# Four column orders for the streamed operand and the PSUM tile of the dense layers, chosen by chunk

## The chip, the cores and the metric

The kernel runs on one core of one Trainium2 chip. The metric is the device time of one launch in microseconds (us), the median of several executions. TensorE (PE in the profile) multiplies matrices, VectorE (DVE), ScalarE (ACT) and GpSimd (POOL) work on rows, and 16 DMA engines move data. A matmul on PE is two instructions: a weight load (LDWEIGHTS, PEld in the profile) puts one operand into the array, and the matmul streams the other operand past it, column by column, and adds the products up in a tile of PSUM.

## What is computed

Two layers of linear attention and two dense layers alternate on one sequence of 2048 rows with 576 features. The change touches the dense layers only, which the reference writes so:

```
def _B_ref(x, w1, b1, w2, b2):
    h = jnp.einsum("bsd,df->bsf", x, w1) + b1
    zero = jnp.zeros_like(h)
    r = jnp.where(h > zero, h, zero)
    h = r * r
    out = jnp.einsum("bsf,fd->bsd", h, w2) + b2
    return out
...
    x = x + _A_ref(_layernorm(x, axis=-1), A_wqkv, A_w_phi, A_wo)
    x = x + _B_ref(_layernorm(x, axis=-1), B_w1, B_b1, B_w2, B_b2)
```

The two lines at the end are run twice. w1 is 576 x 4608, w2 is 4608 x 576.

## The kernel before

The sequence is cut into four blocks of 512 rows (TB). For each layer and block the generator `g_mlp` computes the dense layer, eight times in all. It goes through the 4608 hidden features in NF = 36 chunks of 128, numbered f.

For precision every operand is held as a high and a low part in the type fp32r, and a product is summed from three matmuls (high by high, low by high, high by low). For chunk f this gives 29 matmuls:

- `hidden(f, cols)`, L979, 14 matmuls: the weights are a 128 x 128 piece of w1, the streamed operand is 128 x 512 of the normalised rows, transposed (`x["h"]`, `x["l"]`). They add up in the PSUM tile `ph` (named m_0ph to m_3ph by block), 128 x 512. In the first block of a layer (`apart`), chunks 0 and 1 are done in two halves of 256 columns.
- `square(f)`, L991 to L997: ACT adds the bias, clips and squares `ph` into `hr`, DVE splits the result into the high and low part `hb`.
- `by_rows(f, ts)`, L1017, 12 matmuls: for each of four row tiles t the weights are 128 x 128 of `hb`, and the streamed operand is 448 columns (R) of the chunk's rows of w2 (`s2`). They add up over all 36 chunks in the PSUM tile `acc[t]`.
- `features(f)`, L1005, 3 matmuls with 512 columns: the remaining 128 of the 576 output columns, into the fifth tile `acc[KC]`. The change does not touch them.

In the steady part the order on PE is hidden(f), then by_rows(f-1) and features(f-1), so that `square(f)` runs while PE does the products of the chunk before. Between two chunks `weave` lets pieces of the next block's attention in. Each engine takes its instructions in the order in which the program was written (`manual_schedule`), and the weights arrive by DMA from SP's queue one chunk ahead.

Three matmuls outside the dense layers matter below, since their operands aren't one unbroken run of columns. L587 (`kv_tile`) streams `zeros`, eight runs of 36 columns that all read the same 36 values, into an unbroken output of 288 columns. L617 (`key_totals`) streams two runs of 18 columns and writes two runs of 18; L611 beside it streams and writes 126 in one run. L494 (`project`) has 288 columns in one run.

Of the kernel before, what the change touches and what calls it, by code (L numbers as in the profile page):

```python
# [21 lines left out]
def layers_kernel(  # L22
# [18 lines left out]
    nc = tc.nc  # L41
# [7 lines left out]
    KC = D // P  # L49
# [864 lines left out]
    def g_mlp(layer, b, x, after, name, fresh, apart, final):  # L914

        acc, parts, raw2 = [], {}, {}
        R = D - P
# [41 lines left out]
        def bank(f):  # L959
            parts[f] += (ps_w.tile([P, TB], F32, tag="w", name=f"{name}ph{f}") if f == 1 else  # L960
                         ps_a.tile([P, TB], F32, tag="h", name=f"{name}ph{f}"),)

        def hidden(f, cols):
            if len(parts[f]) == 3:
                bank(f)
            h1, l1, s2, ph = parts[f][:4]
            xh, xl = x["h"], x["l"]
            todo = []
            for c in range(NC):
                ops = [(0, h1[:, c], xh[:, c, cols]), (1, l1[:, c], xh[:, c, cols])]  # L970
                if c < KC:
                    ops.insert(1, (0 if cols == every else 2, h1[:, c], xl[:, c, cols]))
                if c == KC and cols != every:
                    ops = [(3, *op[1:]) for op in ops]
                todo += ops
            if fresh or cols != every:
                todo.sort(key=lambda op: op[0])
            for k, (_, a, m) in enumerate(todo):
                nc.tensor.matmul(ph[:, cols], a, m, start=(k == 0), stop=(k == 3 * KC + 1))  # L979

        def square(f, cols=None, by_act=True):
            if len(parts[f]) == 4:
# [24 lines left out]
        def by_rows(f, ts):  # L1007
            if len(parts[f]) == 3:
                s2, hh, hl = parts[f]
            else:  # L1010
                s2, hb = parts[f][2], parts[f][5]
                hh, hl = hb[:, :TB], hb[:, TB : 2 * TB]
            hi, lo = s2[:, :R], s2[:, D : D + R]
            for t in ts:
                rows = slice(t * P, (t + 1) * P)
                for k, (a, m) in enumerate(((hh, hi), (hh, lo), (hl, hi))):
                    nc.tensor.matmul(acc[t][:, :R], a[:, rows], m, start=(f == 0 and k == 0),  # L1017
                                     stop=(f == NF - 1 and k == 2))

        def sums():  # L1020
# [2 lines left out]
        def second(f):  # L1023
            if not acc:
                sums()
            by_rows(f, range(NT // 2 if apart and f == 0 else 0, NT))
            features(f)
            del parts[f]

        halves = (slice(0, TB // 2), slice(TB // 2, TB))  # L1030
        if apart:
            if fresh:
                for f in range(3):
                    load(f)
            for f in range(2):
                first(f, nc.gpsimd)
                first2(f, nc.gpsimd)
            yield
            for f in range(2):
                hidden(f, halves[0])  # L1040
                if f == 0:
                    square(0, halves[0], False)
                yield
            sums()
            by_rows(0, range(NT // 2))
            for f in range(2):
                hidden(f, halves[1])
                square(f, None if f else halves[1])
            yield
            yield  # L1050
        else:
            for f in range(2):
                first(f)
                first2(f)
                hidden(f, every)
                square(f)
                yield
# [7 lines left out]
        for f in range(2, NF):  # L1065
            if fresh and f + 2 < NF:
                load(f + 2)
            if f + 1 < NF:
                first(f + 1)
            hidden(f, every)  # L1070
            square(f)
            yield
            if final and f == NF - 1:
                features(f - 1)
                by_rows(f - 1, range(NT - 1))
            else:
                second(f - 1)
            if f + 1 < NF:
                first2(f + 1)
            yield  # L1080
# [404 lines left out]
    def body():  # L1485
# [3 lines left out]
        for layer in range(2):  # L1489
            q1 = None  # L1490
            ready, prev_rows, keep = {}, None, {}
            for i, b in enumerate(order):
                n = f"{layer}_{b}"
                nxt, rows = {}, []
                gen = g_mlp(layer, b, ready, rows, f"m{n}", layer == 0 and i == 0, i == 0, layer == 1 and i == NB - 1)
                plan = Plan()
                if i == 0:
# [115 lines left out]
```

## Time and profile before

| what | value |
|---|---|
| median of three runs | 2489.95 us (2489.04 to 2490.05) |
| the profiled execution, its own time | 2489.11 us |
| its span, first to last instruction | 2487.4 us |
| outside the span | 1.7 us |
| PE weight load busy | 2177.9 us (88%) |
| DVE, ACT, POOL busy | 1275.0, 792.1, 307.6 us |
| DMA, mean share and rate | 59.5% in the hardware queue, 220 GB/s of HBM reads and writes |

A row of a view names line, engine, operation, output and inputs, shape and count; then the busy time in us, the mean duration of one in ns, and the idle time before. PE's durations overlap: a matmul's row runs on while the next one has begun, so what a matmul costs is the step from its start to the next start, and the duration is longer than that. In the view in order of time, neighbours with the same names are merged into one row with a count. A shape 128\*128 128x512 is 128 weight rows and columns, and a streamed operand of 128 partitions with 512 columns.

### The profile page before, as it was taken

Reading aid. Unit: us, or ns where it says so; the run is one execution under the profiler, and the core shown is the slowest. Engines: PE = TensorE matmul, PEld = TensorE weight load, DVE = VectorE, ACT = ScalarE, POOL = GpSimd, SP = SyncE. Lnnn points to the kernel's source line nnn. Section 1 sums busy time; section 2 is a strip of 40 time slices with the busy share of each in tenths; the row PEclk is TensorE's granted clock in tenths of the full one; section 3 lists DMA queues with packets and bytes.
Section 4 is the critical chain, followed back from the end, with each engine's and each line's share of the span. In section 5 each row is a group of like instructions: output and inputs, shape, how many; then the busy total and the mean of one; then the engine's idle time right before and its main releaser. Section 6 shows DMA issues by size and latency. Waiting matters only on the chain.

```text
span 2487.4 us, 37668 instructions
## 1 busy us (share of the span) xinstructions
PE 2472.3 (99%) x14924; PEld 2177.9 (88%) x14924; DVE 1275.0 (51%) x2234; ACT 792.1 (32%) x1439; POOL 307.6 (12%) x709
## 2 busy tenths in 40 slices
PE   9999999999999999999999999999999999999999
PEld 8999888889888888888888988888888888888887
DVE  6678885545744476455113776433553436442112
ACT  5444553423232223233223332312232222312212
POOL 4211210110302112020000022010110103020000
PEclk9999999999999999999999999999999999999999
DMA  9312698996767677595555248668576767666555
GB/s 318 102 54 92 238 310 276 318 339 214 259 234 274 222 235 265 208 325 169 194 197 172 97 152 271 207 216 289 178 256 210 259 222 244 218 225 232 194 198 170
DMA packets 177733, 550.57 MB, mean 221 GB/s; under 512 B 24302, under 2 KB 54478, under 8 KB 177558
## 3 DMA queue, kind: packets, MB, share of 16 engines
q1 hardware_dynamic: 163638, 500.44, 59.5%
q0 software_dynamic: 13920, 47.72, 5.9%
q8 instruction: 118, 1.93, 0.3%
q14 instruction: 57, 0.47, 0.1%
HBM read 441.95 MB, written 106.14 MB: 220 GB/s over the span
## 4 chain that ended last, share of the span: by engine, by line
PE 92%; DMA 3%; DVE 2%; POOL 1%; ACT 1%; issue 1%; SPq 0%; DVEq 0%; POOLq 0%; ACTq 0%
PE m_1ph L979 9%; PE m_2ph L979 9%; PE m_0ph L979 9%; PE m_3ph L979 8%; PE m_1acc L1017 7%; PE m_2acc L1017 7%; PE m_0acc L1017 7%; PE m_3acc L1017 6%; PE m_2acc L1005 2%; PE m_1acc L1005 2%; PE m_0acc L1005 2%; PE m_3acc L1005 2%; PE a_0po L817 1%; PE a_2po L817 1%; DMA a_1e<-phs 1%; PE kvp L594 1%
## 5 line engine op out<-in xcount | busy, mean ns | idle before, releaser
L979 PE MATMUL m_2ph<-a_2nh,m_2h 128*128 128x512 f32 x720 | 224.3, 393 | 2.2 <-DMA m_2h<-dw 2.2
L979 PE MATMUL m_0ph<-a_0nh,m_0h 128*128 128x512 f32 x720 | 224.2, 393 | 0.0
L1017 PE MATMUL m_0acc<-m_0s,m_0hb 128*128 128x448 f32 x864 | 189.4, 367 | 0.1
L1017 PE MATMUL m_3acc<-m_3s,m_3hb 128*128 128x448 f32 x864 | 189.4, 367 | 0.0
L1017 PE MATMUL m_1acc<-m_1s,m_1hb 128*128 128x448 f32 x864 | 189.2, 367 | 0.0
L1017 PE MATMUL m_2acc<-m_2s,m_2hb 128*128 128x448 f32 x864 | 189.0, 367 | 0.0
L996 DVE CAST m_2hb<-m_2hr 128x512 fp32r<-128x512 f32 x72 | 31.1, 432 | 287.9 <-ACT m_2hr L992 287.9
L1017 PEld LDWEIGHTS m_1acc<-m_1s,m_1hb 128*128 128x128 f32 x864 | 161.8, 188 | 18.0
L1017 PEld LDWEIGHTS m_0acc<-m_0s,m_0hb 128*128 128x128 f32 x864 | 161.3, 188 | 17.8 <-DVE m_0hb L997 0.8
L1017 PEld LDWEIGHTS m_3acc<-m_3s,m_3hb 128*128 128x128 f32 x864 | 161.3, 188 | 17.3
L1017 PEld LDWEIGHTS m_2acc<-m_2s,m_2hb 128*128 128x128 f32 x864 | 161.4, 188 | 17.1
L979 PEld LDWEIGHTS m_2ph<-a_2nh,m_2h 128*128 128x128 f32 x720 | 135.2, 188 | 33.5 <-issue 2.6
L996 DVE CAST m_1hb<-m_1hr 128x512 fp32r<-128x512 f32 (+1 forms) x73 | 30.9, 423 | 259.2 <-ACT m_1hr L992 259.1
L979 PEld LDWEIGHTS m_0ph<-a_0nh,m_0h 128*128 128x128 f32 x720 | 135.2, 188 | 30.6
L991 ACT ACTIVATE m_2hr<-m_2ph,b1t 128x512 f32<-128x512 f32 x72 | 49.6, 689 | 337.8 <-PE m_2ph L979 331.3
L991 ACT ACTIVATE m_1hr<-m_1ph,b1t 128x512 f32<-128x512 f32 (+1 forms) x72 | 49.4, 686 | 322.1 <-PE m_1ph L979 317.2
L991 ACT ACTIVATE m_0hr<-m_0ph,b1t 128x512 f32<-128x512 f32 x72 | 49.6, 689 | 312.1 <-PE m_0ph L979 312.1
L996 DVE CAST m_0hb<-m_0hr 128x512 fp32r<-128x512 f32 x72 | 31.4, 436 | 211.6 <-ACT m_0hr L992 211.5
L991 ACT ACTIVATE m_3hr<-m_3ph,b1t 128x512 f32<-128x512 f32 (+1 forms) x72 | 49.3, 685 | 213.0 <-PE m_3ph L979 213.0
L996 DVE CAST m_3hb<-m_3hr 128x512 fp32r<-128x512 f32 (+1 forms) x73 | 32.2, 441 | 163.9 <-ACT m_3hr L992 163.9
L979 PE MATMUL m_3ph<-t0onh,m_3h 128*128 128x512 f32 (+1 forms) x380 | 112.9, 384 | 0.7 <-ACT m_3hr L991 0.4
L979 PE MATMUL m_0ph<-a_0nl,m_0h 128*128 128x512 f32 x288 | 113.2, 393 | 0.0
(2089 smaller groups left out, 5861.6 us busy)
## 6 DMA issues: line engine op xcount, KB each, us to landing
m_2h<-dw SPq DMA_DIRECT2D x72, 640.0 KB
m_0h<-dw SPq DMA_DIRECT2D x72, 640.0 KB
m_1h<-dw SPq DMA_DIRECT2D x72, 640.0 KB
m_2s<-dw SPq DMA_DIRECT2D x72, 576.0 KB
m_0s<-dw SPq DMA_DIRECT2D x72, 576.0 KB
m_1s<-dw SPq DMA_DIRECT2D x72, 576.0 KB
dw<-m_3h SPq DMA_DIRECT2D x36, 640.0 KB
m_3h<-dw SPq DMA_DIRECT2D x36, 640.0 KB
```

The costliest lines, as they stand in the source:

```text
L594: nc.tensor.matmul(po[32 * q : 32 * q + 32, :, j], vt[:, h * VW : h * VW + 32], e[:, :, h * DH : (h + 1) * DH], start=not stay, stop=True, ...
L817: nc.tensor.matmul(pt[:, :HP], a, m[:w, g], start=(g == 0 and k == 0), stop=(g == NG - 1 and k == 2))
L979: nc.tensor.matmul(ph[:, cols], a, m, start=(k == 0), stop=(k == 3 * KC + 1))
L991: nc.scalar.activation(hr[:, cols], ph[:, cols], AF.Relu, bias=b1t[:, f : f + 1])
L996: nc.vector.tensor_copy(hh[:, cols], hr[:, cols])
L1005: nc.tensor.matmul(acc[KC], a, m, start=(f == 0 and k == 0), stop=(f == NF - 1 and k == 2))
L1017: nc.tensor.matmul(acc[t][:, :R], a[:, rows], m, start=(f == 0 and k == 0), stop=(f == NF - 1 and k == 2))
```

## The change

A new function `walk` gives a view of a tile with its columns in another order. `hidden` and `by_rows` apply it to the streamed operand and to the PSUM tile alike, so each product still lands in its own column. The order goes by the chunk, f // 2 % 4:

- 0 (f = 0, 1, 8, 9, ...; 10 of the 36 chunks): forwards, as before.
- 1 (f = 2, 3, 10, 11, ...; 10 chunks): backwards, from the last column to the first.
- 2 (f = 4, 5, 12, 13, ...; 8 chunks): four columns from the first half, four from the second half, and so on.
- 3 (f = 6, 7, 14, 15, ...; 8 chunks): the same with sixteen columns.

```
+        def walk(f, v):
+            way = f // 2 % 4
+            if way == 1:
+                return v[:, ::-1]
+            if way == 2:
+                return v.rearrange("p (h g c) -> p g h c", h=2, c=4)
+            if way == 3:
+                return v.rearrange("p (h g c) -> p g h c", h=2, c=16)
+            return v
...
-                nc.tensor.matmul(ph[:, cols], a, m, start=(k == 0), stop=(k == 3 * KC + 1))
+                nc.tensor.matmul(walk(f, ph[:, cols]), a, walk(f, m), start=(k == 0), stop=(k == 3 * KC + 1))
...
-                    nc.tensor.matmul(acc[t][:, :R], a[:, rows], m, start=(f == 0 and k == 0),
+                    nc.tensor.matmul(walk(f, acc[t][:, :R]), a[:, rows], walk(f, m), start=(f == 0 and k == 0),
```

No instruction is added, removed or put elsewhere on any engine; lines after `walk` move down by ten (L979 becomes L989, L1005 L1015, L1017 L1027).

The first place is on PE in the first block (m_3), where chunk 5's hidden products end, chunk 4's row products follow, and chunk 6 begins; `m_3s` is w2's chunk, `m_3hb` the squared hidden part, and the last number but one in a name such as m_3s_4_4120 is the chunk. Before:

```order
L979 MATMUL m_3ph_4207<-t0onh,m_3h_5_4134 128x512 x6
L1017 MATMUL m_3acc_3933<-m_3s_4_4120,m_3hb_4154 128x448 x3
L1017 MATMUL m_3acc_3934<-m_3s_4_4120,m_3hb_4154 128x448 x3
L1017 MATMUL m_3acc_3935<-m_3s_4_4120,m_3hb_4154 128x448 x3
L1017 MATMUL m_3acc_3936<-m_3s_4_4120,m_3hb_4154 128x448 x3
L1005 MATMUL m_3acc_3937<-m_3hb_4154,m_3s_4_4120 128x512 x3
L979 MATMUL m_3ph_4265<-t0onh,m_3h_6_4203 128x512
```

and with the change, in the same rows:

```order
L989 MATMUL m_3ph_4207<-t0onh,m_3h_5_4134 128x64x2x4 x6
L1027 MATMUL m_3acc_3933<-m_3s_4_4120,m_3hb_4154 128x56x2x4 x3
L1027 MATMUL m_3acc_3934<-m_3s_4_4120,m_3hb_4154 128x56x2x4 x3
L1027 MATMUL m_3acc_3935<-m_3s_4_4120,m_3hb_4154 128x56x2x4 x3
L1027 MATMUL m_3acc_3936<-m_3s_4_4120,m_3hb_4154 128x56x2x4 x3
L1015 MATMUL m_3acc_3937<-m_3hb_4154,m_3s_4_4120 128x512 x3
L989 MATMUL m_3ph_4265<-t0onh,m_3h_6_4203 128x16x2x16
```

The order of the rows is the same; only the shapes differ. 64x2x4 is 64 times two runs of 4 columns, 56x2x4 the same for 448 columns, 16x2x16 is 16 times two runs of 16. A backward chunk prints the shape it had before.

The second place is the start of the second block's dense layer (m_2) on PE, at the first row products, with what each row waits for: DMAHW is a transfer, DVE and PE an instruction of that engine. Before:

```order
L979 MATMUL m_2ph_6241<-a_2nh,m_2h_1_6237 128x512 x3
L1017 MATMUL m_2acc_6281<-m_2s_0_6214,m_2hb_6232 128x448 [waits DMAHW6_49,DVE_49]
L1017 MATMUL m_2acc_6281<-m_2s_0_6214,m_2hb_6232 128x448 [waits DVE_49]
L1017 MATMUL m_2acc_6282<-m_2s_0_6214,m_2hb_6232 128x448 x3
L1017 MATMUL m_2acc_6283<-m_2s_0_6214,m_2hb_6232 128x448 x3
```

and with the change:

```order
L989 MATMUL m_2ph_6241<-a_2nh,m_2h_1_6237 128x512 x3
L1027 MATMUL m_2acc_6281<-m_2s_0_6214,m_2hb_6232 128x448 [waits DMAHW6_49,DVE_49,PE_49]
L1027 MATMUL m_2acc_6281<-m_2s_0_6214,m_2hb_6232 128x448 [waits DVE_49]
L1027 MATMUL m_2acc_6282<-m_2s_0_6214,m_2hb_6232 128x448 [waits PE_49]
L1027 MATMUL m_2acc_6282<-m_2s_0_6214,m_2hb_6232 128x448 x2
L1027 MATMUL m_2acc_6283<-m_2s_0_6214,m_2hb_6232 128x448 [waits PE_49]
```

The matmul that opens a sum in a tile now also waits for an earlier instruction of its own engine. Over the whole program 33 rows of PE get such a wait and 12 lose one; on the other engines no row and no wait differs.

## The prediction

> **What bounds the kernel now.** I read the page first: the busy shares, the clock row and the chain that ended last.
>
> ```profile
> PE 2472.3 (99%) x14924; PEld 2177.9 (88%) x14924; DVE 1275.0 (51%) x2234; ACT 792.1 (32%) x1439; POOL 307.6 (12%) x709
> ...
> PEclk9999999999999999999999999999999999999999
> ...
> PE 92%; DMA 3%; DVE 2%; POOL 1%; ACT 1%; issue 1%; SPq 0%; DVEq 0%; POOLq 0%; ACTq 0%
> PE m_1ph L979 9%; PE m_2ph L979 9%; PE m_0ph L979 9%; PE m_3ph L979 8%; PE m_1acc L1017 7%; PE m_2acc L1017 7%; PE m_0acc L1017 7%; PE m_3acc L1017 6%; PE m_2acc L1005 2%; PE m_1acc L1005 2%; PE m_0acc L1005 2%; PE m_3acc L1005 2%; PE a_0po L817 1%; PE a_2po L817 1%; DMA a_1e<-phs 1%; PE kvp L594 1%
> ```
>
> PE is busy 99% of the span at a granted clock of nine tenths or more in every slice, and 92% of the chain is PE. The two lines that the change edits, L979 and L1017, hold 9+9+9+8 and 7+7+7+6, that is 62% of it. No other engine stands close behind. So what one of these matmuls costs, from its start to the next start, passes straight into the time, with nothing to hide a loss and nothing to absorb a gain.
>
> The view of PE in order of time gives that step, here in a stretch of two chunks where nothing else is let in.
>
> ```profile
> 1503.72 0.86 PE L1005 MATMUL m_1acc<-m_1hb,m_1s 128*128 128x512 f32 x3
> 1504.41 0.40 PE L979 MATMUL m_1ph<-t1onh,m_1h 128*128 128x512 f32 x1
> 1504.65 0.39 PE L979 MATMUL m_1ph<-t1onl,m_1h 128*128 128x512 f32 x1
> ...
> 1507.68 2.63 PE L1017 MATMUL m_1acc<-m_1s,m_1hb 128*128 128x448 f32 x12
> 1510.15 0.87 PE L1005 MATMUL m_1acc<-m_1hb,m_1s 128*128 128x512 f32 x3
> 1510.86 0.39 PE L979 MATMUL m_1ph<-t1onh,m_1h 128*128 128x512 f32 x1
> ...
> 1514.05 1.18 PE L1017 MATMUL m_1acc<-m_1s,m_1hb 128*128 128x448 f32 x5
> ```
>
> The 14 hidden products take 1507.68 - 1504.41 = 3.27 us in one chunk and 1514.05 - 1510.86 = 3.19 us in the next: a step of 0.234 or 0.228 us for 512 columns. The 12 row products take 2.47 us, 0.206 us each for 448 columns. A chunk is 6.45 us here.
>
> How much of a step is columns? Two shapes of one group tell it:
>
> ```profile
> L979 PE MATMUL m_1ph<-t1onh,m_1h 128*128 128x512 f32 x340 | 106.1, 393 | 0.3 <-DMA m_1h<-dw 0.3
> L979 PE MATMUL m_1ph<-t1onh,m_1h 128*128 128x256 f32 x40 | 6.2, 288 | 0.2 <-DVE t1onh L396 0.2
> ```
>
> 256 columns more make a matmul 393 - 288 = 105 ns longer: 0.41 ns per column. So 512 columns are 0.210 us of the 0.228 to 0.234 us, and some 0.02 us per matmul is something else that this trace doesn't name.
>
> **The change, part by part.** It adds, removes and moves no instruction. What it alters is the order in which 26 matmuls of a chunk (14 + 12) read one operand and write PSUM, in 26 of 36 chunks: 10 backwards, 8 in runs of four, 8 in runs of sixteen. Over eight dense layers that is 80 + 64 + 64 = 208 chunks and 208 x 26 = 5408 matmuls. The sum is 5408 times what another order costs, and one ns per matmul is 5.4 us, or 0.2% of the time.
>
> First, **broken runs on the side that is read**. One matmul of the kernel already reads in eight runs, L587, and it happens to start with its weight load still to be waited for. So I compare it with an L494 of the same 288 columns, in one run, that starts the same way; rows of the loads and of the matmuls in order of time, then the durations (min, median, max):
>
> ```profile
> 56.45 0.18 PEld L587 LDWEIGHTS kvp<-zero 1*128 1x128 f32 x1 [0.17 <-issue]
> 56.45 0.40 PE L587 MATMUL kvp<-zero 1*128 1x288 f32 x1
> ...
> 58.09 0.19 PEld L494 LDWEIGHTS f0q0p<-t0q0h,n_0h 128*128 128x128 f32 x1
> 58.09 0.40 PE L494 MATMUL f0q0p<-t0q0h,n_0h 128*128 128x288 f32 x1
> ...
> L587 PE MATMUL kvp<-zero x2: 393/396/398, 56.5 to 1347.3; 1*128 1x288 f32 x2
> L494 PE MATMUL f0q0p<-t0q0h,n_0h x3: 294/295/400, 58.1 to 59.0; 128*128 128x288 f32 x3
> ```
>
> Both start together with their load, and last 393 to 398 ns against 400 ns. Seven jumps back cost nothing that shows within 5 ns. Had the broken runs halved the rate, 288 columns would have been 288 x 0.41 = 118 ns longer. That is the nearest row for the two interleaved orders; its limits are that the runs have 36 columns and not 4 or 16, that it uses one row of the array, and that its output is in one run. If a jump cost as much as a column, these 7 would be 3 ns and not seen.
>
> Second, **broken runs on the side that is written**. L617 writes two runs of 18 columns, L611 beside it 126 in one run:
>
> ```profile
> L611 PE MATMUL z<-kv,top x32: 273/275/275, 216.1 to 1417.2; 128*128 128x126 f32 x32
> L617 PE MATMUL z<-kv,top x16: 200/279/279, 217.9 to 1418.0; 128*128 128x36 f32 x16
> ```
>
> The shortest L617 is 275 - 200 = 75 ns shorter for 90 columns less, 0.83 ns per column: no extra shows. But that type runs at twice the time per column of L979, so a cost that needs full rate to appear could hide there. I take nothing for the interleaved orders; the upper bound is double the column time, below.
>
> Third, **the backward order**. No operand in this trace has a descending step, on either side. The bounds are nothing and double the column time, which is the price L617 and L611 pay per column. I take nothing, because a backward walk has no jump at all (each column is the neighbour of the one before), so it lies nearer to the unbroken rows than L587 does, and L587 was free.
>
> Fourth, **33 rows of PE that newly wait for PE, and 12 that no longer do**. Such waits exist before; one is the attention transpose below (its row of the program waits for PE alone).
>
> ```profile
> 349.82 0.63 PE L1005 MATMUL m_3acc<-m_3hb,m_3s 128*128 128x512 f32 x2
> 350.29 0.27 PE L773 MATMUL a_2pt<-ident,a_2Q2e 128*126 128x128 f32 x1
> ```
>
> It starts 350.29 - 349.82 = 0.47 us after the first of two matmuls, the usual two steps, so it waited for nothing. The new waits open a sum in a tile whose last writer lies some matmuls back, and I cost them at nothing. If each instead let the pipeline run empty it would pay duration less step, 0.39 - 0.23 = 0.16 us: 33 x 0.16 = 5 us above, and 12 x 0.16 = 2 us below for those that go. Queued behind such a row is all of PE, and behind PE the `square` on ACT and DVE, which have half their time free.
>
> Fifth, **the 0.02 us per matmul that isn't columns**. Two neighbouring chunks with the same shapes take 3.27 and 3.19 us, so this part isn't fixed, and another order may move it. If all 208 reordered chunks took the longer of the two, half of them would lose 0.08 us: 104 x 0.08 = +8 us; if all took the shorter, -8 us. I take zero, between them.
>
> The sum is 2489.1 us for the profiled execution (its span of 2487.4 and 1.7 around it) plus nothing; that execution lies 0.8 us under the median, so I say 2490 for the median, and its own range by the fourth and fifth part is -8 - 2 to +8 + 5: about 2479 to 2503 us.
>
> **The rivals.**
>
> *Backwards at half rate; this one makes it slower.* If PE takes descending columns one at a time where it takes ascending ones two at a time (a doubling as between L979's and L617's column), L979 and L1017 pay 0.41 ns per column more: 14 x 512 x 0.41 = 2.9 us and 12 x 448 x 0.41 = 2.2 us, 5.1 us per chunk, and with 80 chunks 408 us: 2897 us. If the 0.02 us disappears behind the slower columns, 26 x 0.02 = 0.5 us per chunk comes off: 2857 us. For it: no row shows a descending step free. Against it: only that it has no jumps. It decides from 5 us / (80 x 26) = 2.4 ns per matmul on.
>
> *Everything that isn't a plain ascending run at half rate.* 208 x 5.1 = 1061 us: 3550 us. L587 and L617 speak against it, the one on the read side, the other on the written side. [...]
>
> *A jump costs a column.* Runs of four have 127 jumps in 512 columns and 111 in 448: (14 x 127 + 12 x 111) x 0.41 = 1.3 us per chunk, 64 chunks 82 us; sixteens have 31 and 27 jumps, 0.3 us per chunk, 20 us. Together 2489 + 102 = 2591 us. Or only the runs of four run at half rate: 64 x 5.1 = 326 us, 2815 us. L587's spread of 5 ns can't rule out the first.
>
> *Faster.* If the 0.02 us per matmul comes from two readers that meet in step, another order may part them; the whole of it on 5408 matmuls is 108 us, but the only variation that the trace shows is the 0.08 us per chunk: 2481 us.
>
> **How the numbers follow.** My forecast, no price for any order, gets 0.58; backwards at half rate 0.22; everything at half rate 0.10; a price for jumps or for the runs of four 0.10. A measurement of this kernel can tell about 0.2%, 5 us, from no change. Within the forecast the 8 us either way reach beyond that, so I split its 0.58 into 0.34 same, 0.12 faster and 0.12 slower. That gives faster 0.12, same 0.34, slower 0.12 + 0.22 + 0.10 + 0.10 = 0.54. The likeliest case is 2490 us with its own range of 2479 to 2503. The range that should hold it 8 times in 10 must take in the backward rival up to 2897, and with it the prices of jumps; only everything at half rate is left out: 2478 to 2900 us.
>
> **What would show it.** Right: in the groups that keep shapes apart, the 512-column and the 64x2x4 or 16x2x16 forms of L989 have one mean near 393 ns, and L1027's near 367 ns; in order of time a chunk stays at 3.2 to 3.3 and 2.5 us, whichever f it has. Backwards slow: chunks 2, 3, 10, 11 and so on take some 6.1 us for the 14, the others 3.2. Jumps priced: chunks with runs of four longest, sixteens a quarter of that. The waits: idle time with PE as its end at the first L1027 of a block. I am wrong if any order differs from the forward one by more than 3 ns per matmul.

## The result and the profile after

| | before | after |
|---|---|---|
| median | 2489.95 us on record; 2490.0 us (2489.04 to 2491.94) with the runs beside the change | 2531.91 us (2529.34 to 2535.05), four runs |
| the profiled execution, its own time | 2489.11 us | 2535.05 us |

The ratio of the times is 1.0168, with a 95% interval of 1.0153 to 1.0182: the change costs 42 us. First the page of the changed kernel: its span, the busy shares, the chain that ended last, and the two groups that answer to L979 and L1017 (busy us, mean ns of one, idle us before).

```profile
span 2533.3 us, 37668 instructions
PE 2518.1 (99%) x14924; PEld 2188.5 (86%) x14924; DVE 1277.6 (50%) x2234; ACT 794.9 (31%) x1439; POOL 304.6 (12%) x709
...
PE 97%; DVE 1%; DMA 1%; ACT 0%; issue 0%; SPq 0%; DVEq 0%; ACTq 0%
...
L989 PE MATMUL m_2ph<-a_2nh,m_2h 128*128 128x512 f32 x720 | 231.0, 403 | 2.2 <-DMA m_2h<-dw 2.2
...
L1027 PE MATMUL m_2acc<-m_2s,m_2hb 128*128 128x448 f32 x864 | 192.8, 372 | 0.0
```

The busy share of PE is the 99% that it was, the row groups show no idle time before them, and the counts agree with before's. Only the mean durations differ. These are the two groups in the kernel before:

```profile
L979 PE MATMUL m_2ph<-a_2nh,m_2h 128*128 128x512 f32 x720 | 224.3, 393 | 2.2 <-DMA m_2h<-dw 2.2
...
L1017 PE MATMUL m_2acc<-m_2s,m_2hb 128*128 128x448 f32 x864 | 189.0, 367 | 0.0
```

393 ns became 403, and 367 became 372. Summed over the whole trace, each matmul taken from its start to the next start, the hidden products went from 933.8 to 964.0 us and the row products from 708.5 to 723.6: 30.3 + 15.0 = 45.3 us of the 45.9 us by which the span grew. All other lines together make up the remaining 0.6 us.

The mean hides which order pays. The profile prints one shape, 128x512, for all four orders, so the groups can't tell them apart, as I had thought they would. The view of PE in order of time can, since the chunks come in the order of f. Here are chunks 27 (backwards), 28 and 29 (fours) and 30 (sixteens) of block m_1 in the first layer; the columns are the start of the first matmul, busy us, and the rows of the program. Each chunk's hidden products stand first, then the row products of the chunk before.

```profile
1303.89 0.39 PE L989 MATMUL m_1ph<-a_1nh,m_1h 128*128 128x512 f32 x1
...
1307.16 2.64 PE L1027 MATMUL m_1acc<-m_1s,m_1hb 128*128 128x448 f32 x12
1309.64 0.85 PE L1015 MATMUL m_1acc<-m_1hb,m_1s 128*128 128x512 f32 x3
1310.33 0.41 PE L989 MATMUL m_1ph<-a_1nh,m_1h 128*128 128x512 f32 x1
...
1313.84 2.64 PE L1027 MATMUL m_1acc<-m_1s,m_1hb 128*128 128x448 f32 x12
1316.31 0.85 PE L1015 MATMUL m_1acc<-m_1hb,m_1s 128*128 128x512 f32 x3
...
1320.51 2.73 PE L1027 MATMUL m_1acc<-m_1s,m_1hb 128*128 128x448 f32 x12
1323.07 0.86 PE L1015 MATMUL m_1acc<-m_1hb,m_1s 128*128 128x512 f32 x3
1323.77 0.40 PE L989 MATMUL m_1ph<-a_1nh,m_1h 128*128 128x512 f32 x1
...
1327.13 2.73 PE L1027 MATMUL m_1acc<-m_1s,m_1hb 128*128 128x448 f32 x12
1329.69 0.87 PE L1015 MATMUL m_1acc<-m_1hb,m_1s 128*128 128x512 f32 x3
```

The 14 hidden products take 1307.16 - 1303.89 = 3.27 us backwards, 1313.84 - 1310.33 = 3.51 us in fours, and 1327.13 - 1323.77 = 3.36 us in sixteens. The 12 row products of a chunk in fours take 1323.07 - 1320.51 = 2.56 us, those of a backward chunk 1316.31 - 1313.84 = 2.47. The next table has the same reading over all chunks, from the start times in the trace: medians over the chunks of one order (even and odd chunks apart, then averaged, since they differ, as before's 3.19 and 3.27 us show).

| order | 14 hidden products | step | 12 row products | step |
|---|---|---|---|---|
| all chunks before | 3231 ns | 230.8 ns | 2456 ns | 204.7 ns |
| forwards | 3226 | 230.4 | 2458 | 204.8 |
| backwards | 3268 | 233.4 | 2478 | 206.5 |
| fours | 3506 | 250.4 | 2560 | 213.3 |
| sixteens | 3359 | 239.9 | 2546 | 212.2 |

Every order but the forward one has a price. With the chunks of each: fours 64 x (275 + 104) ns = 24.3 us, sixteens 64 x (128 + 90) = 14.0 us, backwards 80 x (37 + 22) = 4.7 us, together 43.0 of the 45.3 us. Medians leave out what happens in chunks into which other work is let. Taken chunk by chunk, each against the same chunk before, the sums are 24.1 us for fours, 14.3 for sixteens, 6.3 for backwards and 0.7 for forwards, which makes the whole 45.3.

The averages hide one thing about the backward order. Before, an even chunk took 3196 ns and an odd one 3266; backwards they take 3266 and 3271. So a backward chunk takes what an odd forward chunk took, and the 37 ns are 70 in the even chunks and 5 in the odd ones. Fours and sixteens (3507 and 3505; 3357 and 3362) are dearer in both.

### The profile page after: what moved, and what is told of

It is laid out like the page before. It is cut to its first block, busy times and chain, and to the rows that moved or that the text cites. A ratio compares the mean times of both kernels' runs of the same rounds, so it can differ in the third digit from the quotient of the medians.

```text
span 2533.3 us, 37668 instructions
## 1 busy us (share of the span) xinstructions
PE 2518.1 (99%) x14924; PEld 2188.5 (86%) x14924; DVE 1277.6 (50%) x2234; ACT 794.9 (31%) x1439; POOL 304.6 (12%) x709
## 4 chain that ended last, share of the span: by engine, by line
PE 97%; DVE 1%; DMA 1%; ACT 0%; issue 0%; SPq 0%; DVEq 0%; ACTq 0%
PE m_0ph L989 9%; PE m_3ph L989 9%; PE m_2ph L989 9%; PE m_1ph L989 9%; PE m_0acc L1027 7%; PE m_1acc L1027 7%; PE m_3acc L1027 7%; PE m_2acc L1027 7%; PE m_0acc L1015 2%; PE m_3acc L1015 2%; PE m_2acc L1015 2%; PE m_1acc L1015 2%; PE a_2po L817 1%; PE a_0po L817 1%; PE kvp L594 1%; PE a_3po L817 1%
## 5 line engine op out<-in xcount | busy, mean ns | idle before, releaser
L989 PE MATMUL m_2ph<-a_2nh,m_2h 128*128 128x512 f32 x720 | 231.0, 403 | 2.2 <-DMA m_2h<-dw 2.2
L989 PE MATMUL m_0ph<-a_0nh,m_0h 128*128 128x512 f32 x720 | 229.9, 401 | 0.0
L1027 PE MATMUL m_0acc<-m_0s,m_0hb 128*128 128x448 f32 x864 | 193.0, 373 | 0.5 <-issue 0.5
L1027 PE MATMUL m_3acc<-m_3s,m_3hb 128*128 128x448 f32 x864 | 193.2, 373 | 0.0
L1027 PE MATMUL m_1acc<-m_1s,m_1hb 128*128 128x448 f32 x864 | 192.9, 372 | 0.0
L1027 PE MATMUL m_2acc<-m_2s,m_2hb 128*128 128x448 f32 x864 | 192.8, 372 | 0.0
L1027 PEld LDWEIGHTS m_1acc<-m_1s,m_1hb 128*128 128x128 f32 x864 | 162.4, 189 | 21.5
L1027 PEld LDWEIGHTS m_0acc<-m_0s,m_0hb 128*128 128x128 f32 x864 | 161.9, 188 | 21.4 <-issue 0.9
L1027 PEld LDWEIGHTS m_2acc<-m_2s,m_2hb 128*128 128x128 f32 x864 | 162.0, 188 | 20.6
L1027 PEld LDWEIGHTS m_3acc<-m_3s,m_3hb 128*128 128x128 f32 x864 | 161.9, 189 | 20.6
L989 PEld LDWEIGHTS m_2ph<-a_2nh,m_2h 128*128 128x128 f32 x720 | 136.9, 190 | 37.6 <-issue 2.6
L989 PEld LDWEIGHTS m_0ph<-a_0nh,m_0h 128*128 128x128 f32 x720 | 136.0, 189 | 34.4
L989 PE MATMUL m_2ph<-a_2nl,m_2h 128*128 128x512 f32 x288 | 116.3, 404 | 0.0
L989 PE MATMUL m_1ph<-t1onh,m_1h 128*128 128x512 f32 (+1 forms) x380 | 115.0, 390 | 0.8 <-DMA m_1h<-dw 0.6
```

Source lines behind the costliest of these rows:

```text
L989: nc.tensor.matmul(walk(f, ph[:, cols]), a, walk(f, m), start=(k == 0), stop=(k == 3 * KC + 1))
L1027: nc.tensor.matmul(walk(f, acc[t][:, :R]), a[:, rows], walk(f, m), start=(f == 0 and k == 0), stop=(f == NF - 1 and k == 2))
```

## The experiments

Four questions were open: whether the price lies with the streamed operand or with PSUM; whether it is one price per matmul, per jump, or by the distance jumped; whether the weight load that runs beside each matmul has a part in it; and whether an order exists that gains. In the experiments with many orders the tiles carry the order's name (m_2fourph is a `ph` of a chunk in fours), so that the groups do tell them apart. "Step" is the time from one matmul's start to the next, the mean over all chunks of the order in the trace unless it says otherwise. The runs are told by question here. Those of all sides, lengths, fewer weight columns and backwards in all chunks shared a chip, where before's median was 2491.04 us; those of one side, distance and re-reading had another (2490.32), the search a third (2491.05), and the last three, kept weights and the two versions that gain, a fourth (2490.23).

### Each side alone

Nine ways take turns by f // 2 % 9: forwards, fours, sixteens or backwards on the read side alone (r), on the written side alone (w), and fours and sixteens on both.

```
WAYS = ("f", "rq", "rs", "rb", "wq", "ws", "wb", "q", "s")
...
def walk(f, v, side):
    way = WAYS[f // 2 % 9]
    if len(way) == 2 and way[0] != side:
        return v
...
nc.tensor.matmul(walk(f, ph[:, cols], "w"), a, walk(f, m, "r"), start=(k == 0), stop=(k == 3 * KC + 1))
```

> The chunks take turns in nine ways, two chunks each: forwards; streamed operand alone in another order (fours, sixteens, backwards; the PSUM tile forwards); PSUM tile alone in another order (the same three); both in fours; both in sixteens. Where only one side is walked the products land in other columns, so it is no longer the dense layer. In the changed kernel a hidden product steps 228 to 233 ns forwards, 233 backwards, 250 in fours, 240 in sixteens, and a row product 204 to 206, 206, 213, 212. Theory R (the reads of the streamed operand meet the reads of the next weight load in SBUF): the read-only chunks step as with both sides walked, 250, 240 and 213, the write-only chunks as forwards. Theory W (the cost is in the writes to PSUM): the write-only chunks step 250, 240 and 213, the read-only ones as forwards. Theory S (a broken pattern costs each matmul a fixed start, whichever side): both show some +8 ns.

The time was 2525.43 us. The groups of the second block's hidden products:

```profile
L998 PE MATMUL m_2rfourph<-a_2nh,m_2h 128*128 128x512 f32 x80 | 26.8, 417 | 1.3 <-DMA m_2h<-dw 1.3
L998 PE MATMUL m_2fourph<-a_2nh,m_2h 128*128 128x512 f32 x80 | 26.6, 416 | 0.0
L998 PE MATMUL m_2rsixteenph<-a_2nh,m_2h 128*128 128x512 f32 x80 | 25.8, 404 | 0.0
L998 PE MATMUL m_2rbackph<-a_2nh,m_2h 128*128 128x512 f32 x80 | 25.3, 398 | 0.0
L998 PE MATMUL m_2wbackph<-a_2nh,m_2h 128*128 128x512 f32 x80 | 24.9, 392 | 0.0
L998 PE MATMUL m_2wfourph<-a_2nh,m_2h 128*128 128x512 f32 x80 | 24.9, 392 | 0.0
L998 PE MATMUL m_2wsixteenph<-a_2nh,m_2h 128*128 128x512 f32 x80 | 24.9, 392 | 0.0
L998 PE MATMUL m_2fwdph<-a_2nh,m_2h 128*128 128x512 f32 x80 | 24.6, 393 | 0.0
```

The three written ways last 392 ns, as long as forwards; fours on the read side alone last 417, as long as on both (416). The steps say the same: hidden and row 251.3 and 214.0 ns for read fours against 230.6 and 203.6 for written fours. The price is on the read side, whole.

### The read side and the written side over a whole kernel

The changed kernel's orders, walked on one side only; the other side is left forwards.

```
way = f // 2 % 4 if side == "r" else 0
...
way = f // 2 % 4 if side == "w" else 0
```

> The change on the streamed operand alone; PSUM is written forwards, so products land in other columns and it is no longer the dense layer. If all of the change's cost is on the read side: as the changed kernel, 2532 us (2527 to 2537). If PSUM had a share that showed only with both: less.

> The change on the PSUM tile alone; the streamed operand is read forwards, so it is no longer the dense layer. If all of the cost is on the read side: as before the change, 2490 us (2486 to 2494). If broken writes cost anything: above 2495.

Reading alone took 2531.3 us (2529.69 to 2534.49), ratio 1.0168 (1.0153 to 1.0183): all that the change costs. Writing alone took 2490.14 us (2486.09 to 2492.61) beside 2490.32, ratio 1.000 (0.9991 to 1.001): nothing. The group of the hidden products in the kernel that walks on the written side alone:

```profile
L989 PE MATMUL m_2ph<-a_2nh,m_2h 128*128 128x512 f32 x720 | 224.2, 393 | 0.3 <-DMA m_2h<-dw 0.3
```

393 ns, the number before. The new waits of PE for PE come with the walk over PSUM (by the traces 30 row products wait for an instruction of PE in this run and in the changed kernel, 6 before the change and in the read-only run), so this run prices them too: nothing that can be measured.

### Length of the runs, number of the jumps

Forwards; the two halves swapped (one jump); pieces of 128 and 112 columns from the two halves in turn (three jumps); runs of 2, 8 and 32 from the halves; runs of 4 from four quarters (`quart`) and from eight eighths (`octet`); backwards. All on both sides.

```
if way == "h":
    return v.rearrange("p (h c) -> p h c", h=2)[:, ::-1]
if way == "n4":
    return v.rearrange("p (h g c) -> p g h c", h=2, g=2)
if way[0] == "c":
    return v.rearrange("p (h g c) -> p g h c", h=2, c=int(way[1:]))
if way[0] == "p":
    return v.rearrange("p (h g c) -> p g h c", h=int(way[1:]), c=4)
```

> Both sides are walked, two chunks each: forwards; second half before first (one jump); halves interleaved in a quarter of the columns (three jumps); by 2; by 8; by 32; quarters interleaved by 4; eighths interleaved by 4; backwards. Theory S (fixed start per broken pattern): every broken order steps some 8 ns more, 236 to 241 ns for a hidden product, whatever the number of jumps. A price per jump: by 2 costs twice what fours cost (+40 ns or more, 270), by 8 half of it (+10), by 32 and the single jump next to nothing. Theory R (two readers meet in SBUF, so addresses decide): no rule by the number of jumps; quarters and eighths by 4 differ from halves by 4 though they jump as often, and the price stays below some 40 ns for runs of 8 and longer.

The time was 2616.80 us. Groups of the second block, hidden and then row products:

```profile
L998 PE MATMUL m_2twoph<-a_2nh,m_2h 128*128 128x512 f32 x80 | 33.3, 501 | 0.0
L998 PE MATMUL m_2octetph<-a_2nh,m_2h 128*128 128x512 f32 x80 | 28.9, 444 | 0.0
L998 PE MATMUL m_2quartph<-a_2nh,m_2h 128*128 128x512 f32 x80 | 28.1, 435 | 0.0
L998 PE MATMUL m_2eightph<-a_2nh,m_2h 128*128 128x512 f32 x80 | 26.0, 407 | 0.0
L998 PE MATMUL m_2thirtyph<-a_2nh,m_2h 128*128 128x512 f32 x80 | 25.4, 398 | 0.0
L998 PE MATMUL m_2bigph<-a_2nh,m_2h 128*128 128x512 f32 x80 | 25.0, 394 | 0.0
L998 PE MATMUL m_2fwdph<-a_2nh,m_2h 128*128 128x512 f32 x80 | 24.6, 392 | 0.0
...
L1036 PE MATMUL m_2acc<-m_2s,m_2octethb 128*128 128x448 f32 x96 | 21.0, 368 | 0.0
L1036 PE MATMUL m_2acc<-m_2s,m_2quarthb 128*128 128x448 f32 x96 | 20.9, 365 | 0.0
```

There is no fixed price for an order that isn't forwards: one jump (231.7 ns) and three (231.4) cost about a nanosecond over forwards (230.5). Nor is there a price per jump: runs of four have 127 jumps in every split, yet the hidden step is 250 ns from halves, 267.6 from quarters and 277.4 from eighths. And the same runs of four cost the row products nothing from quarters (204.0 against 203.3) and 2.5 ns from eighths (205.8). What differs between hidden and row is the distance: quarters of 512 columns lie 512 bytes apart, quarters of 448 lie 448 bytes apart. Runs of 2 columns, 8 bytes, are dear in any case (331.9 and 291.4).

### Fewer weight columns

The hidden products have half of the 128 weight columns, so that a hidden product's weight load is shorter (135 ns on average in place of 189); the upper 64 hidden features of each chunk are left out. The row and feature products then sum over these 64 features only, so their weights are 64 rows by 128 columns in place of 128 by 128.

```
-                nc.tensor.matmul(walk(f, ph[:, cols]), a, walk(f, m), start=(k == 0), stop=(k == 3 * KC + 1))
+                nc.tensor.matmul(walk(f, ph[:64, cols]), a[:, :64], walk(f, m), start=(k == 0), stop=(k == 3 * KC + 1))
```

> The changed kernel with its four orders, but the hidden products load 64 weight columns instead of 128 (the upper 64 hidden features of each chunk are left out of the dense layer). 512 columns are 512 x 0.41 = 210 to 213 ns. Theory R: what a step has beyond its columns belongs to the weight load and halves with it: forwards 228 to 233 becomes 220 to 224, backwards 233 becomes 223, sixteens 240 becomes 227, fours 250 becomes some 232. Theories W and S: the price of an order over forwards stays, +9 for sixteens and +20 for fours, whatever forwards becomes.

The time was 2622.40 us, longer than the changed kernel, because of the seams between products whose weights have 64 rows and products whose weights have more: there the steps of the dense layers' products are some 290 to 330 ns. It is the rows and not the columns. A product of 64 x 128 weights and 512 streamed columns that is followed by one of 128 x 128 has a step of 324 ns, by one of 126 x 126 also 324; a product of 128 x 64 weights followed by the same two has 240 (medians of 23, 24, 8 and 24 steps). Inside a chunk, with the first and last of the 14 left out, the steps are 230.2 ns forwards, 233.5 backwards, 247.2 in fours and 240.0 in sixteens, where the changed kernel has 230.1, 233.4, 250.4 and 240.0 (medians over chunks, even and odd apart, then averaged). The price did not halve: sixteens and backwards pay the same over forwards, fours 17 ns in place of 20.

### Weights that are read from one column

The weight load has its full length, but reads one column 128 times, so that the hidden features of a chunk are all alike.

```
-                nc.tensor.matmul(walk(f, ph[:, cols]), a, walk(f, m), start=(k == 0), stop=(k == 3 * KC + 1))
+                nc.tensor.matmul(walk(f, ph[:, cols]), a[:, :1].to_broadcast([P, P]), walk(f, m),
+                                 start=(k == 0), stop=(k == 3 * KC + 1))
```

> The change with its four orders, but each hidden product's weight load reads one column 128 times, so that it needs one piece of SBUF and not sixteen (the hidden features of a chunk are then all alike; not the dense layer). Theory F's second half (the 15 ns beyond the columns are pieces read for the weight load): forwards falls from 228 to 233 to some 216 to 220, as when the streamed operand's columns were kept, and the prices of the orders fall with it or stay on top (backwards 216 to 222, sixteens 220 to 230, fours 225 to 240). If the stream stalls by itself, whatever the weight load reads: 230, 233, 240, 250 as in the changed kernel.

The time was 2528.68 us. The groups of the second block's hidden products in fours and forwards:

```profile
L992 PE MATMUL m_2fwdph<-a_2nh,m_2h 128*128 128x512 f32 x200 | 62.1, 393 | 0.0
...
L992 PE MATMUL m_2fourph<-a_2nh,m_2h 128*128 128x512 f32 x160 | 53.3, 415 | 0.0
```

The steps inside a chunk, taken as in the run before, were 230.3 forwards, 233.4 backwards, 249.1 in fours and 240.0 in sixteens: the changed kernel's within 1.3 ns. With the run before, this rules out the weight load as the main cause: neither its length nor the addresses it reads move the price of sixteens and backwards by half a nanosecond, and they take at most 3.3 of the 20 ns off that of fours. It isn't wholly without a part, though. The gap between even and odd forward chunks, 4.9 ns per step in the changed kernel (227.7 and 232.6), is 2.8 with one column read (228.9 and 231.7) and gone with 64 columns (230.5 and 230.0).

DMA and DVE run beside the stream too, and the trace of the changed kernel speaks against them as the cause. Of its chunks in fours, the third with the least DMA traffic (the engines busy for a mean share of 0.42) has a hidden step of 250.1 ns, the third with the most (0.92) 250.4. The third in which DVE is idle and the third in which it is busiest (0.86) both have 250.2. For sixteens all four are 240.0.

### Backwards in all chunks

```
-            way = f // 2 % 4
...
+            return v[:, ::-1]
```

> All 36 chunks of every dense layer backwards, both sides. In the changed kernel a backward chunk is 37 ns longer in its 14 hidden products and 21 ns in its 12 row products than the same chunk before (medians of the pairs of chunks). If that is the price of the backward order itself: 288 x 0.058 = +17 us, 2507 us (range 2500 to 2515). If it is a price of changing from one order to another between chunks, which this kernel never does: 2490 us, as before.

2507.27 us (2506.95 to 2508.95), ratio 1.0071 (1.0054 to 1.0088). 288 chunks at (37 + 22) ns are 17.0 us, and 16.2 were measured. So the price belongs to the backward order itself, 2 to 3 ns per matmul on average, and not to changing from one order to another. It isn't the same in every run: where backwards is one of nine orders its hidden step is some 5 ns above forwards (235.6 against 230.6, read side alone), because its odd chunks often take 237 or 240 ns and not 233. Why, no run shows.

### Distance

Parts of the columns and runs, apart for hidden and row products: runs of 4 from 16, 32 and 64 parts (hidden; 7, 14 and 28 parts for row), and runs of 16, 8 and 2 at several distances.

```
WAYS = (("fwd", 0, 0, 0, 0), ("sixteenth", 16, 4, 7, 4), ("thirtysecond", 32, 4, 14, 4),
        ("sixtyfourth", 64, 4, 28, 4), ("quartsixteen", 4, 16, 4, 16), ("octsixteen", 8, 16, 8, 8),
        ("quarteight", 4, 8, 4, 8), ("octeight", 8, 8, 4, 2), ("quarttwo", 4, 2, 16, 4))
...
return v.rearrange("p (h g c) -> p g h c", h=way[0], c=way[1])
```

> Both sides walked, two chunks each in nine ways, cut into more and fewer parts, so that one run follows the other at another distance. Measured before it, for runs of four (16 bytes): distance 1024 bytes +20 ns per hidden product, 512 bytes +37, 256 bytes +46; in the row products 896 bytes +8, 448 bytes 0, 224 bytes +1. Theory B (SBUF serves neighbouring addresses from several banks, and two runs at a multiple of 128 bytes meet in one bank): hidden at 128 bytes +46 or more (276 to 285 ns), at 64 bytes and at 32 bytes clearly less (under +20, below 250); row products at 256 bytes (seven parts) and 128 bytes (fourteen parts) +35 to +45 (240 to 250 ns), at 64 bytes and at 112 bytes 0 to +10 (204 to 214). Runs of sixteen and of eight in the row products at 448 and 224 bytes are free as well (204 to 208), in the hidden products at 512 and 256 bytes dearer than the halves' +9 and +12. Theory J (what counts is the number of jumps and which operand it is): hidden products with runs of four all +20 to +46 at 128, 64 and 32 bytes, row products with runs of four all 204 to 213, and runs of sixteen and eight in the row products at 448 bytes 210 to 213 as at 896.

The time was 2689.79 us. Groups of the second block:

```profile
L992 PE MATMUL m_2sixteenthph<-a_2nh,m_2h 128*128 128x512 f32 x80 | 26.3, 411 | 0.0
L992 PE MATMUL m_2sixtyfourthph<-a_2nh,m_2h 128*128 128x512 f32 x80 | 25.0, 394 | 0.0
L1030 PE MATMUL m_2acc<-m_2s,m_2sixteenthhb 128*128 128x448 f32 x96 | 24.7, 411 | 0.0
L992 PE MATMUL m_2thirtysecondph<-a_2nh,m_2h 128*128 128x512 f32 x80 | 24.6, 388 | 0.0
L992 PE MATMUL m_2fwdph<-a_2nh,m_2h 128*128 128x512 f32 x80 | 24.6, 392 | 0.0
L1030 PE MATMUL m_2acc<-m_2s,m_2thirtysecondhb 128*128 128x448 f32 x96 | 21.6, 376 | 0.0
L1030 PE MATMUL m_2acc<-m_2s,m_2fwdhb 128*128 128x448 f32 x96 | 20.8, 365 | 0.0
L1030 PE MATMUL m_2acc<-m_2s,m_2sixtyfourthhb 128*128 128x448 f32 x96 | 20.6, 362 | 0.0
```

A `sixteenth` chunk has its hidden parts 128 bytes apart and its row parts 256 bytes apart; `thirtysecond` 64 and 128; `sixtyfourth` 32 and 64. Together with the runs of four of the earlier experiments, the steps by distance, as the difference from forwards in the same run:

| bytes from one run of four to the next | hidden, ns | row, ns |
|---|---|---|
| 1024 (halves) | +20 | |
| 896 (halves) | | +10 |
| 512, 448 (quarters) | +37 | +1 |
| 256, 224 (eighths) | +47 | +2 |
| 256 | | +40 |
| 128 | +16 | +9 |
| 112 | | +4 |
| 64 | -3 | -3 |
| 32 | +1 | |

The three multiples of 256 bytes that were run are the dear ones (+20 to +47 ns), and among these those that visit more parts before they come back to a neighbour (in the hidden products 20 ns with two parts, 37 with four, 47 with eight). 128 and 896 bytes (896 is 128 less than 1024) cost less (+9 to +16 ns), and the rest little or nothing (-3 to +4). My expectation of +46 and +35 ns at 128 bytes was three to four times too high; that of +35 to +45 for row products at 256 bytes held. Longer runs cost less. In the hidden products at 512 bytes it is 2 ns for runs of 8 and 3 for runs of 16, less than the 13 and 10 from halves, which I had expected the other way; at 256 bytes it is 19 and 10. Runs of 2 from quarters are the dearest order of all, 449.5 and 386.3 ns.

### What is kept of what was read

The streamed operand re-reads its first c columns over and over, so that the other columns are left out of the products. PSUM is written forwards.

```
return v[:, :c].unsqueeze(1).to_broadcast([P, n // c, c])
```

> The streamed operand is a few columns read again and again (4, 8, 16, 32, 64, a quarter, a half), two chunks each, beside forwards and backwards (these alone are walked on the read side only); PSUM forwards; it is no longer the dense layer. [...] Theory J (jumps): the price goes with the number of jumps back: 4 columns as fours or more (250), 16 columns 240, 64 and more as forwards.

The time was 2479.07 us. Groups of the second block's hidden products (four, eight, ... is c):

```profile
L994 PE MATMUL m_2sixteenph<-a_2nh,m_2h 128*128 128x512 f32 x80 | 25.6, 402 | 0.0
L994 PE MATMUL m_2thirtytwoph<-a_2nh,m_2h 128*128 128x512 f32 x80 | 25.5, 400 | 0.0
L994 PE MATMUL m_2sixtyfourph<-a_2nh,m_2h 128*128 128x512 f32 x80 | 24.9, 393 | 0.0
L994 PE MATMUL m_2fwdph<-a_2nh,m_2h 128*128 128x512 f32 x80 | 24.6, 392 | 0.0
L994 PE MATMUL m_2fourph<-a_2nh,m_2h 128*128 128x512 f32 x80 | 24.0, 381 | 1.3 <-DMA m_2h<-dw 1.3
L994 PE MATMUL m_2eightph<-a_2nh,m_2h 128*128 128x512 f32 x80 | 23.9, 379 | 0.0
```

There is an edge between 8 and 16 columns. Re-reading 4 or 8 columns gives a step of 215.8 ns inside a chunk, under every value I had expected; 16 columns give 240, more than reading all 512 (230.5), and 32 columns 238; from 64 on it is the forward step within a nanosecond. The row products have the same edge: 190.0 for 4 and 8 columns, 212 for 16, 203 forwards. So a plain forward step is some 15 ns longer than one that stays within 8 columns, 32 bytes (230.5 - 215.8). My guess was that a piece of what was read is kept at the reader; the run shows the prices and no piece, and the edge lies somewhere between 32 bytes (215.8 ns) and 64 bytes (240 ns).

### A search near 64 bytes

Runs of 8, 4 and 2 at 64 bytes (`h = n // 16`), some with the parts in descending order; neighbouring pieces of 8 swapped; fours wholly backwards; pieces of 8 in descending order.

```
w = v.rearrange("p (h g c) -> p g h c", h=v.shape[-1] // 16, c=c)
```

> Orders that visit the operand in steps of 64 bytes (16 columns), both sides walked, two chunks each: forwards; runs of eight; runs of four; the same two with the steps descending; neighbouring eights swapped; runs of four wholly backwards; runs of two; eights in descending order with their columns ascending. Two chunks of the run before had runs of four at 64 bytes: 228 ns per hidden product against 230 forwards, 201 per row product against 204. Reading 4 or 8 columns again and again took 215 and 190, 64 and more as forwards: theory F, SBUF is read in pieces of 32 bytes (eight columns) from eight banks in turn; an order stalls where one piece meets a bank too soon after another, and forwards loses some 15 ns to pieces read for something else, the weight load being the one reader beside it. By it runs of eight at 64 bytes are at least as good as runs of four (228 or below, 201 or below), swapped eights and eights in descending order cost about as forwards or backwards (228 to 236), and runs of two at 64 bytes, which need each piece four times, cost far more (over 280). Rival N: the 64-byte result is the spread between chunks (223 and 229, 196 and 204 in its two chunks) and not the order: runs of four and eight scatter around 228 to 233 and 203 to 206 here.

The time was 2672.21 us. Groups of the second block:

```profile
L998 PE MATMUL m_2swappedph<-a_2nh,m_2h 128*128 128x512 f32 x80 | 27.9, 432 | 0.0
L998 PE MATMUL m_2eightph<-a_2nh,m_2h 128*128 128x512 f32 x80 | 25.2, 396 | 0.0
L998 PE MATMUL m_2fourph<-a_2nh,m_2h 128*128 128x512 f32 x80 | 24.7, 389 | 0.0
L998 PE MATMUL m_2fwdph<-a_2nh,m_2h 128*128 128x512 f32 x80 | 24.6, 393 | 0.0
```

Fours at 64 bytes are again faster than forwards, 228.0 and 200.2 ns against 230.7 and 203.4, with another neighbour in the list than in the distance run, so the gain is probably the order's own; the next experiment tests it on the whole kernel. By the guess of a piece of 32 bytes, runs of eight at 64 bytes had to be at least as good; they are slower (233.6 and 204.7). Swapped pieces were to take 228 to 236 ns and took 266.8. Two expectations held: pieces in descending order were to take 228 to 236 ns and took 234.1, and runs of two were to take over 280 and took 433.2.

### A version that beats both

The walk in fours at 64 bytes in every chunk; then in `features` and in the two lines of the attention's projections as well (L494, L817), where `by64` is the same walk. The first line below is both versions', the others the second's.

```
return v.rearrange("p (h g c) -> p g h c", h=v.shape[-1] // 16, c=4)
...
nc.tensor.matmul(walk(f, acc[KC]), a, walk(f, m), start=(f == 0 and k == 0), stop=(f == NF - 1 and k == 2))
...
nc.tensor.matmul(by64(pt[:, :HP]), a, by64(m), start=(k == 0), stop=(k == 3 * KC + 1))
```

> The dense layers' hidden and row products all in runs of four columns at steps of 64 bytes, both sides walked. If the gain of that order in the two runs before (228.0 against 230.7 ns per hidden product, 200.2 against 203.4 per row product) is the order's own: 288 x (14 x 2.7 + 12 x 3.2) ns = -22 us, 2468 us (2462 to 2474). If it was the place of those chunks in the round of nine: 2490 us, as before.

> As the run in fours at 64 bytes, and the same order for the dense layers' three feature products, the attention's projections of 288 columns (L494 of before) and its output products (L817 of before). 864 feature products at -2.7 ns and 3648 others at about -2: another -9 us, 2459 us (2450 to 2468). If the gain depends on the 512- and 448-column operands: 2468 or more.

In the dense layers 2464.74 us (2464.28 to 2466.64), ratio 0.9902 (0.9887 to 0.9917) to the kernel before; with the other lines 2453.15 us (2452.94 to 2456.88), ratio 0.9854 (0.9837 to 0.9870). Groups of the first of the two:

```profile
L982 PE MATMUL m_2ph<-a_2nh,m_2h 128*128 128x512 f32 x720 | 223.0, 391 | 2.2 <-DMA m_2h<-dw 2.2
...
L1020 PE MATMUL m_2acc<-m_2s,m_2hb 128*128 128x448 f32 x864 | 185.7, 362 | 0.0
```

By start times the hidden products are 10.4 us shorter than before and the row products 13.0: 23.4 of the span's 2487.4 - 2463.0 = 24.4 us. So the gain is the order's own, in every chunk. In the second version the projections give another 7.1 us. It lies 6 us under the 2459 us that I expected, inside the range that I gave.

## Why the prediction was right or wrong

The measured 2531.91 us lies in the range of 2478 to 2900 us and on the side that had the larger chance. The likeliest case, no price for any order, with its own 2479 to 2503 us, did not come about. That the range holds the result is luck in part: it reached so far up for the backward order at half rate, which fell, and no rival's own time (2591 us for the jumps, 2815 and more for the half rates) is the measured one. By the prediction's own parts:

- **What bounds the kernel** was right. Each nanosecond on these two lines passed into the time: 45.3 us more on them, 45.9 us more span, and no wait grew to absorb any of it.
- **First, broken runs on the read side: this step failed.** I took no price, from L587, and the two interleaved orders cost 20 and 9 ns (fours, hidden and row) and 9 and 8 ns (sixteens), beyond the 3 ns per matmul that I had named as the point from which I am wrong: 24.3 + 14.0 = 38.3 us. The limit that I gave for L587, the length of its runs, was one reason why it says little: at 32 columns per run the price is already down to 6 and 4 ns. The second I hadn't seen: a jump has a distance, and L587's all go back to the same 36 columns (144 bytes), while the halves of the change lie 1024 and 896 bytes apart. The distance experiments show that for runs of four this decides (-3 to +47 ns per matmul by distance). The third is how little L587 could resolve. Re-reading 32 columns, the nearest thing to it, costs 238.0 - 230.5 = 7.5 ns for 15 jumps; seven jumps at that price are an estimated 3 to 4 ns, inside the 5 ns that my comparison could see. So L587 was never shown to be free.
- **Second, broken runs on the written side: right, on a weak row.** Only the shortest L617 (200 ns) is shorter than L611; its median of 279 lies above L611's 275, so the 0.83 ns per column, and the doubling that I took from it as a bound, are hardly shown by these rows. The experiment settles it: written alone, all orders cost 1.000 (0.9991 to 1.001) of the time before.
- **Third, backwards: nearly right.** Not nothing but 2 to 3 ns per matmul, 16.2 us if all chunks go backwards. On average it stays under those 3 ns in the changed kernel (5 ns in the even chunks' hidden products, next to nothing in the odd ones), and far from a doubling (some 210 ns).
- **Fourth, the waits: right.** The kernel that writes in these orders and reads forwards ran in before's time.
- **Fifth, the 0.02 us per matmul that isn't columns.** The guess that another order may move it was right, its size was not. I bounded it by the spread between two neighbouring chunks, 8 us either way, and in its place the reordered products lost 45 us here (the same 45 us as above) and give 25 us with runs of four at 64 bytes. For the hidden products of the backward chunks the bound was the right one: they all take the longer of the two times. The re-reading run shows that the larger part of the 0.02 us lies with how the stream is read: 230.4 - 215.8 = 15 ns go when it stays within 8 columns.

Of the rivals, the half rates fell: no order of the change costs near 0.41 ns per column more (the dearest, fours, 20 ns over 512 columns, is 0.04). "A jump costs a column" had the sign and the order of the prices right (fours dearer than sixteens), but not the rule: it gave fours 127 x 0.41 = 52 ns where 20 were measured, sixteens 13 ns against 9, and it knows no distance. "Faster, another order may part two readers that meet" did not happen with the change's orders. As for the other reader, the weight load was tried in two ways and isn't the main cause (at most 3.3 of the 20 ns of fours), and neither DMA traffic nor DVE moves the price (fours at 250.1 and 250.4 ns with the least and the most traffic, at 250.2 with DVE idle and busiest).

What stays open: why the price goes as it does. My guess in the search, pieces of 32 bytes read from eight banks in turn, was made from the prices; no run shows a piece or a bank. It fits which distances are dear for the runs of four in the table, but it does not explain why 1024, 512 and 256 bytes cost 20, 37 and 47 ns, why eights at 64 bytes lose 3 ns, why swapped neighbours lose 36, or why even and odd chunks differ by 70 ns with the same order (3196 and 3266 ns before).

## What to carry to other kernels

Where TensorE is the bound, the order in which the streamed operand is read is worth a look of its own: here it moved the time from -1.5% to +1.7% with no instruction added, and runs of two columns from quarters nearly doubled the step (449.5 ns against 230.4). The number of jumps didn't decide here; the dear orders were runs of four columns at 256, 512 and 1024 bytes (+20 to +47 ns in the hidden products), runs of two at every distance tried (331.9 to 449.5 ns there), and swapped pieces of eight (266.8 ns). The order in PSUM was free in the forms tried, backwards and runs of four and sixteen (1.000 of the time before), so a layout that needs such a result can have it on the written side. Before a row of the trace is taken as the price of something new, compare every property in which the two differ, the distance as well as the length and the count.

## What the runs showed of the hardware

Three things I had not expected. Re-reading a few columns makes the step of 512 columns 216 ns while they are 4 or 8, and 240 when they are 16, where a forward stream takes 230. A forward stream is not the fastest order that reads every column once (231 and 203 ns against 228 and 200). And a product with 64 rows of weights followed by one with 126 or 128 rows took a step of 324 ns for 512 streamed columns, where a forward step inside a chunk took 230.2; a product with 128 rows and 64 weight columns, followed by the same, took 240.
